# Clearing step 5's zero rows on VectorE, and a new order for the first batch

## The chip, the cores and the metric

The kernel runs on one core of a Trainium2 chip. The metric is the device time of one execution in microseconds (us), as a median of several runs. The core has five engines, each with its own queue of instructions that it works off in order: TensorE (PE), VectorE (DVE), ScalarE (ACT), GpSimd (POOL) and SyncE (SP). SP, ACT and POOL also issue transfers (DMAs) between the chip's memory and the core. An engine waits where the next instruction in its queue needs something that another engine or a transfer has not delivered yet.

## The reference

The program is an attention with normalised q and k, whose output goes through a layer of eight experts to which tokens are routed by a hash of their id.

```python
q_n = q / sqrt(mean(q*q) + 1e-6) * g_q        # q, k, v: 8 x 12 x 448 x 64
k_n = k / sqrt(mean(k*k) + 1e-6) * g_k
attn = softmax(q_n @ k_n^T / sqrt(64))
x = attn @ v                                   # as 3584 x 768
expert = token_id * 2654435761 % 8
out[mask_e] = relu(x[mask_e] @ w1[e]) @ w2[e]  # for each expert e
```

## The kernel before

Attention comes first, then the experts. Attention has 48 steps: eight batches of six, and each step takes two heads. The 448 tokens of a head lie as 64 rows of seven, and the two heads of a step share the 128 partitions. The seven groups of 64 keys of two heads make three full blocks of scores (j = 0, 1, 2) and a half one (j = 3).

Around the steps stands the preparation, by groups of steps. In the first batch, group 0 is step 0 alone, group 1 the pair of steps 1 and 2, group 2 the pair 3 and 4 and step 5 alone. The work is written as short tokens, `kind:step.part` or `kind:group.tensor`, that a Python loop turns into instructions. Nothing reorders them: each engine's queue is the order of the tokens that it takes part in. The kinds are:

- `sqq`, `sqk`: squares of q or k of a group. `sumq`, `sumk`: partial sums of them on PE. `redq`, `redk`: the rest of the sums on DVE. `ln`, `er`: two ACT operations that turn the sums into 1/rms, for k and q of a group together, or apart for group 0 (`ln:0.0.1` is q's, `ln:0.1.2` is k's).
- `nq`, `nk`: DVE multiplies q or k by 1/rms (lines 420 to 440). `Tq`, `Tk`: PE transposes the result into a PSUM bank. `qT`, `kT`: that bank is copied to SBUF, kT with the factor g_col.
- `sc`: scores on PE. `exp`: exponentials on ACT. `av`: product with v on PE, in three parts. `rec`, `x`: reciprocal of the row sums and the final product on DVE. `v`: a copy of a chunk of v on DVE.
- `zero`: clears rows that no load fills. `spin`: PE multiplies zeros, with no result used. `gain`: the factors g_q and g_k are made into g_col.

A suffix says who does it or where: `@A` puts a square or a copy on ACT instead of DVE; `@S` puts sums or transposes into a bank of the ring of three that the scores use, instead of the one bank of their own.

Odd heads leave holes in the blocks of a single step, so for steps 0 and 5 some rows of q and k are cleared. For step 5 `zero:3` does it on ACT, in two copies of zeros, and then issues six small loads on SP (four for k, two for q, in 32 bits, without a cast) and the load of the token ids. Step 0's k comes on SP's and ACT's queues; all other loads of q, k and v are issued by POOL in the order of its queue, and but for step 0's q they change 32 bits to 16.

The first string of tokens covers batch 0 and batch 1 up to `exp:12.2`; a second string, `steady`, is then emitted for each batch from 2 on and begins with `exp:12.3` for batch 2. The names in the rows: `first` is shown as expT, whose buffer it borrows; `raw(1, 5)` and `raw(0, 5)` are parts of kr and qr; `warm`, the zeros, is shown as hi.

Of the kernel before, what the change touches and what calls it, by code (L numbers as in the profile page):

```python
# [20 lines left out]
def kernel(  # L21
# [12 lines left out]
    nc = tc.nc  # L34

    B, H, S, D = q.shape
# [3 lines left out]
    P = 128  # L40
    HP = H // 2
# [87 lines left out]
    def setup1():  # L129
        tid_t32 = _dc.replace(moe_token_ids.tensor, shape=[N * 2], dtype=I32)  # L130
        nc.sync.dma_start(out=tid32[:],
                            in_=bass.AP(tensor=tid_t32, offset=0,
                                        ap=[[2 * NTC, P], [2, NTC], [1, 2]]))
# [130 lines left out]
    with tc.manual_schedule(), \  # L264
# [45 lines left out]
        def raw_at(bufs, b, o, n):  # L310
            o += RAW // 2 * (b % 2)
            return bufs[b // 2 % NB][:, o:o + n]
# [15 lines left out]
        def raw(a, s):  # L328
            b, i = s // HP, s % HP
            bufs = (q_bufs, k_bufs)[a]  # L330
            if s == 0:
                return first[:, a]
            if s == HP - 1:
                return raw_at(bufs, 0, 4 * PAIR, 16 * D).bitcast(FP32).rearrange(
                    "p (s d) -> p s d", d=D)
            if b == 0:
                t = raw_at(bufs, 0, (i - 1) * PAIR, 2 * PAIR)
                return t.rearrange("p (i s d) -> p i s d", i=2, d=D)
            t = raw_at(bufs, b, 0, 6 * PAIR).rearrange("p (i u s d) -> p u i s d", i=2, u=3, d=D)
            return t[:, i // 2]  # L340
# [107 lines left out]
        V = nc.vector  # L448
# [12 lines left out]
        warm = hi[:].rearrange("p c a h -> p (c a h)")[:, 0:512]  # L461
# [270 lines left out]
        def load_one(s):  # L732
            load_heads([nc.sync] * 4, raw(1, s)[:, None], k, s, 1)
            load_one_q([nc.sync] * 2, raw(0, s), s)

        def zero_q(eng, t):
            eng.memset(t[64:P, 3::4, :], 0.0)

        def zero_kv(eng, t, s0=0, s1=7):
            eng.memset(t[64:P, :, s0, :], 0.0)  # L740
            eng.memset(t[0:64, :, s1, :], 0.0)

        def zero(part):
            V = nc.vector
            if part == 0:
                zero_kv(V, first[:, 1:2])
                zero_q(V, first[:, 0])
            elif part == 1:
                V.memset(n8_one[:, 4, 1], 0.0)
                V.memset(n8_one[:, 8, 0], 0.0)  # L750
            elif part == 2:
                V.memset(n8_k[:, :, 0, 1], 0.0)
                V.memset(n8_k[:, :, 7, 0], 0.0)
            elif part == 3:
                z = warm[:, 0:4 * D].rearrange("p (s d) -> p s d", d=D)
                nc.scalar.copy(raw(1, HP - 1)[:, 0::7], z[:, 0:2])
                nc.scalar.copy(raw(0, HP - 1)[64:P, 3::4], z[64:P, 0:2])
                load_one(HP - 1)
                setup1()
            elif part == 6:  # L760
                zero_kv(V, v_bufs[0])
            elif part == 7:
                V.memset(v8_all[:, :, :, :, D], 1.0)
                V.memset(v8_all[64:P, :, :, 0, D], 0.0)
                V.memset(v8_all[0:64, :, :, 7, D], 0.0)
# [77 lines left out]
        def gain(part):  # L843
            if part == 1:
                pend["g"] = ps_sc.tile([P, 2, 512], FP32, name="sc_ps")[:, 1, 0:1]
            g_mul(part, pend.get("g"))

        setup_ops = {"zero": zero, "gain": gain, "spin": spin}

        flag = ""  # L850

        def emit(text, b):
            nonlocal flag
            g0, s0, c0 = (0, 0, 0) if b is None else (b + 3, HP * b, 2 * b)
            for token in text.split():
                kind, arg = token.split(":")
                kind, _, flag = kind.partition("@")
                at, *rest = [int(a) for a in arg.split(".")]
                if kind in setup_ops:
                    setup_ops[kind](at)  # L860
                elif kind in group_ops:
                    if g0 + at < NG:
                        group_ops[kind](g0 + at, *rest)
                elif kind == "v":
                    if c0 + at < NV:
                        prep_v(c0 + at)
                elif s0 + at < NS:
                    step_ops[kind](s0 + at, *rest)

        emit("""  # L870
            zero:0 zero:1 zero:2 zero:6 zero:7 spin:11 sqk:0.0 zero:3 sqq@A:0.0 sumk@S:0.0
            redk:0.0 sumq@S:0.0 ln:0.1.2 redq:0.0 er:0.1.2 ln:0.0.1 er:0.0.1 sqk@A:1.0
            gain:0 spin:2 nk:0 spin:4 gain:1 Tk@S:0 nq:0 sumk@S:1.0 gain:2 sqq:1.0 Tq@S:0
            redk:1.0 sumq:1.0 kT:0 redq:1.0 qT@A:0 sc:0.0 ln:1 er:1 sc:0.1 spin:5 exp:0.0
            nk:1 Tk@S:1 sc:0.3 nq:1 Tq:1 sqk:2.0.0 kT:1 qT:1 exp:0.1 sqq:2.0.0 v:0
            sqk@A:2.0.1 sc:0.2 exp:0.3 sumk@S:2.0 sc:1.0 sqq@A:2.0.1 exp:0.2 exp:1.0
            sumq:2.0 redk:2.0 av:0.0 redq:2.0 sc:1.2 av:0.1 v:1 sc:1.3 ln:2 er:2 av:0.2
            sc:1.1 nq:3 rec:0 exp:1.2 exp:1.3 Tq@S:3 exp:1.1 nk:3 sc:2.0 Tk:3 x:0 exp:2.0
            sc:2.1 exp:2.1 qT:3 kT:3 sc:2.2 av:1.0 exp:2.2 sc:2.3 av:1.1 av:1.2 sqk:3.0
            sc:4.0 exp:2.3 nk:5 sumk:3.0 rec:1 exp:4.0 sc:3.0 x:1 sc:3.1 av:2.0 redk:3.0  # L880
            av:2.1 sqk:4.0 exp:3.0 nq:5 sumk:4.0 v:2 sc:3.2 av:2.2 redk:4.0 sqq:3.0 rec:2
            exp:3.1 Tk@S:5 sc:3.3 kT:5 x:2 sumq:3.0 exp:3.2 sc:4.3 sc:4.2 exp:3.3 redq:3.0
            exp:4.3 ln:3 er:3 sc:4.1 exp:4.2 av:3.0 sqk:4.1 Tq:5 exp:4.1 sqq:4.0 av:3.1 qT:5
            sumk@S:4.1 nq:6 av:3.2 nk:6 redk:4.1 sc:5.0 rec:3 sumq:4.0 sc:5.3 sc:5.1 exp:5.0
            exp:5.3 redq:4.0 sqq:4.1 x:3 Tk:6 exp:5.1 Tq@S:6 kT:6 sumq@S:4.1 redq:4.1 qT@A:6
            av:4.0 av:4.1 ln:4 sc:5.2 av:4.2 er:4 exp:5.2 sc:6.0 sqk:5.0 v:4 sc:7.0 sumk:5.0
            exp:6.0 rec:4 sc:6.3 x:4 av:5.0 av:5.1 exp:7.0 exp:6.3 nq:8 sc:7.3 redk:5.0 nk:8
            exp:7.3 v:3 Tq:8 sc:6.1 av:5.2 qT:8 sc:6.2 Tk@S:8 rec:5 sqq:5.0 exp:6.1 sc:7.1
            sumq:5.0 x:5 exp:6.2 av:6.0 sc:7.2 exp:7.1 exp:7.2 kT:8 sc:8.0 sqq:5.1 redq:5.0
            sc:8.1 nq:10 exp:8.0 av:6.1 sumq:5.1 nk:10 redq:5.1 exp:8.1 av:6.2 sc:8.3 rec:6  # L890
            Tk:10 x:6 sc:9.0 sc:8.2 exp:8.3 av:7.0 sc:9.3 exp:9.0 kT:10 Tq:10 av:7.1 av:7.2
            sc:9.1 sqk:5.1 qT:10 exp:8.2 rec:7 sc:9.2 x:7 v:5 exp:9.3 exp:9.1 sumk:5.1
            redk:5.1 exp:9.2 sqq:6.0 av:8.0 av:8.1 av:8.2 sc:10.0 sc:10.2 sc:10.1 rec:8 ln:5
            er:5 x:8 nk:12 exp:10.0 sumq:6.0 av:9.0 exp:10.1 sc:10.3 redq:6.0 Tk:12 av:9.1
            nq:12 av:9.2 kT:12 rec:9 exp:10.2 sc:11.0 exp:10.3 exp:11.0 sc:11.2 exp:11.2
            sc:11.3 x:9 Tq:12 sqq:6.1 av:10.0 av:10.1 sc:11.1 qT:12 nk:14 av:10.2 exp:11.3
            sc:12.0 sumq:6.1 sc:12.2 rec:10 exp:11.1 sc:12.1 x:10 exp:12.0 exp:12.2 redq:6.1
            Tk:14 sc:12.3 sqk:6.0 exp:12.1
        """, None)
        steady = """  # L900
            exp:0.3 av:-1.0 av:-1.1 nq:2 av:-1.2 kT:2 sc:1.0 exp:1.0 rec:-1 x:-1 Tq:2 sc:1.1
# [22 lines left out]
    with tc.manual_schedule(), \  # L924
# [116 lines left out]
        V = nc.vector  # L1041
# [236 lines left out]
```

## Time and profile before

| | us |
|---|---|
| median of 3 runs (337.82 to 338.94) | 338.56 |
| the profiled execution | 337.33 |
| its span | 335.8 |
| ACT busy in the span | 188.2 |
| DVE busy in the span | 197.7 |
| start of the first exponential | 11.90 |
| start of the first exponential of the steady part (exp:12.3) | 53.97 |
| start of the last exponential of attention | 157.08 |

The profile is one execution, seen from its span's start at 0. Shares over the whole span mix two stages: attention up to about 158 us, the experts after it. In attention ACT is the engine that the rows show as busy without a break, in the experts it is PE. A row of the timeline is a run of like instructions on one engine: start, time from the first start to the last end, engine and line, operation, what it writes and reads, the shape, how many; in brackets the idle time of the engine just before, and what ended it.

### The profile page before, as it was taken

Reading aid. Unit: us, or ns where it says so; the run is one execution under the profiler, and the core shown is the slowest. Engines: PE = TensorE matmul, PEld = TensorE weight load, DVE = VectorE, ACT = ScalarE, POOL = GpSimd, SP = SyncE. Lnnn points to the kernel's source line nnn. Section 1 sums busy time; section 2 is a strip of 40 time slices with the busy share of each in tenths; the row PEclk is TensorE's granted clock in tenths of the full one; section 3 lists DMA queues with packets and bytes.
Section 4 is the critical chain, followed back from the end, with each engine's and each line's share of the span. In section 5 each row is a group of like instructions: output and inputs, shape, how many; then the busy total and the mean of one; then the engine's idle time right before and its main releaser. Section 6 shows DMA issues by size and latency. Waiting matters only on the chain. (4 is left out here: it accounts for less than half of the span.)

```text
span 335.8 us, 9161 instructions
## 1 busy us (share of the span) xinstructions
PE 322.8 (96%) x3873; PEld 224.9 (67%) x3873; DVE 197.7 (59%) x427; ACT 188.2 (56%) x287; POOL 147.0 (44%) x207
## 2 busy tenths in 40 slices
PE   6899999999999999998999999999999999999992
PEld 3567776777777776666677667677676676766761
DVE  4699999998989899984792342232332323222210
ACT  3799999999999999998442211212022020221211
POOL 8799925423440100003655844538556374203122
PEclk9999999999999999999999999999999999999997
DMA  6999999999999999432587899999999999923012
GB/s 118 205 202 204 214 228 197 242 200 237 203 243 210 248 227 236 84 84 72 156 169 224 162 209 247 264 280 247 255 262 263 268 254 265 267 34 133 25 64 105
DMA packets 45602, 65.54 MB, mean 195 GB/s; under 512 B 12727, under 2 KB 33423, under 8 KB 45432
## 3 DMA queue, kind: packets, MB, share of 16 engines
q0 software_dynamic: 39072, 58.32, 86.0%
q1 hardware_dynamic: 6328, 6.50, 7.2%
q8 instruction: 31, 0.51, 0.6%
q10 hardware_dynamic: 160, 0.11, 0.1%
q14 instruction: 11, 0.09, 0.1%
HBM read 89.29 MB, written 17.30 MB: 317 GB/s over the span
## 5 line engine op out<-in xcount | busy, mean ns | idle before, releaser
L652 ACT ACTIVATE expT<-sc_ps 128x896 bf16<-128x896 f32 x144 | 125.0, 960 | 0.9 <-PE sc_ps L636 0.6
L972 PEld LDWEIGHTS <-h_sb 128*128 128x128 f16 (+1 forms) x512 | 51.3, 104 | 30.2
L972 PE MATMUL o_ps<-w_sb,h_sb 128*128 128x512 f16 (+3 forms) x384 | 66.2, 326 | 0.0
L985 POOL DMA_INDIRECT out_dram<-o_sb,gidx x32 | 33.8, 1055 | 63.4 <-ACT o_sb L982 30.9
L959 ACT ACTIVATE h_sb<-h_ps 128x480 f16<-128x480 f32 (+1 forms) x36 | 19.9, 553 | 67.3 <-PE h_ps L955 67.3
L230 POOL DMA_INDIRECT kr<-x_scratch,gidx x32 | 32.7, 1022 | 50.8 <-DVE oc L578 36.7
L955 PEld LDWEIGHTS <-w_sb 128*128 128x128 f16 x288 | 38.9, 136 | 16.2
L955 PE MATMUL h_ps<-xT,w_sb 128*128 128x480 f16 x240 | 49.4, 366 | 0.0
L982 ACT COPY o_sb<-o_ps 128x768 f32<-128x768 f32 x16 | 12.8, 799 | 60.4 <-PE o_ps L972 55.2
L961 DVE TENSOR_SCALAR h_sb<-h_ps 128x480 f16<-128x480 f32 x28 | 18.4, 658 | 47.2 <-PE h_ps L955 47.2
L636 PE MATMUL sc_ps<-qT,kT 64*128 64x448 f16 x288 | 44.4, 356 | 0.7 <-DVE qT L628 0.4
L671 PEld LDWEIGHTS <-expT 128*128 128x128 bf16 x864 | 37.8, 97 | 9.0 <-DVE x_sb L702 4.1
L671 PE MATMUL av_ps<-v,expT 128*128 128x65 bf16 x846 | 42.3, 193 | 0.1
L982 DVE COPY o_sb<-o_ps 128x768 f32<-128x768 f32 (+1 forms) x15 | 14.3, 956 | 37.1 <-PE o_ps L972 30.3
L305 POOL DMA_DIRECT2D vr<-in_v_dram x36 | 23.7, 669 | 20.1 <-DMA kr<-in_k_dram 10.8
L702 DVE TENSOR_TENSOR x_sb<-av_ps,srec 128x448 f16<-128x448 f32 x47 | 29.2, 622 | 1.3
L655 ACT ACTIVATE expT<-sc_ps 128x448 bf16<-128x448 f32 x48 | 28.6, 599 | 0.1
L386 PEld LDWEIGHTS <-ident 128*128 128x128 f16 x576 | 22.6, 97 | 8.2 <-issue 3.6
L676 PE MATMUL av_ps<-v,expT 128*128 128x130 bf16 x141 | 24.5, 220 | 0.0
L972 PE MATMUL o_ps<-kr,h_sb 128*128 128x512 f16 (+3 forms) x128 | 21.6, 326 | 0.0
L243 DVE COPY xT<-xT_ps 128x768 f16<-128x768 f16 (+1 forms) x21 | 11.0, 524 | 17.9 <-PE xT_ps L242 17.7
L955 PE MATMUL h_ps<-xT,qr 128*128 128x480 f16 x96 | 19.8, 366 | 0.0
(218 smaller groups left out, 437.9 us busy)
## 6 DMA issues: line engine op xcount, KB each, us to landing
w_sb<-in_moe_w_dram POOLq DMA_DIRECT2D x18, 512.0 KB, 12.4
w_sb<-in_moe_w_dram POOLq DMA_DIRECT2D x8, 768.0 KB, 13.1
kr<-in_k_dram POOLq DMA_DIRECT2D x7, 672.0 KB, 14.9
qr<-in_q_dram POOLq DMA_DIRECT2D x7, 672.0 KB, 12.4
x_scratch<-x_sb SPq DMA_DIRECT2D x15, 288.0 KB, 6.8
w_sb<-in_moe_w_dram POOLq DMA_DIRECT2D x2, 1536.0 KB, 21.6
qr<-in_moe_w_dram POOLq DMA_DIRECT2D x6, 512.0 KB, 17.5
vr<-in_v_dram POOLq DMA_DIRECT2D x14, 192.0 KB, 13.1
```

The source lines that it names most:

```text
L230: nc.gpsimd.indirect_dma_start(out=xg[0:idx.shape[0], :], out_offset=None, in_=x_dram[0:rows, :], in_offset=bass.IndirectOffsetOnAxis(ap=i ...
L305: eng.dma_start(out=dst[64 * half:64 * half + 64, :, s0:s0 + cnt, :].rearrange("p n s d -> p n (s d)"), in_=runs(t, h0 + HP * hh, 1, n, to ...
L636: nc.tensor.matmul(sc[:, hh, :S], lhsT=kT[64 * hh:64 * hh + 64, P * j:P * j + P], rhs=qT[64 * hh:64 * hh + 64, :], start=True, stop=True)
L652: nc.scalar.activation(expT[:, 2 * j:2 * j + 2, :], sc[:, :, :S], AF.Exp, bias=0.0, scale=1.0)
L655: nc.scalar.activation(expT[:, 6, :], sc[:, 0, :S], AF.Exp, bias=0.0, scale=1.0)
L671: nc.tensor.matmul(av[:, 2 * t + hh, :], lhsT=expT[:, tl(hh, j), P * t:P * t + P], rhs=v8[:, i, vs(hh, j), 0:D + 1], start=(hh == 0 and t ...
L676: nc.tensor.matmul(av[:, 2 * t:2 * t + 2, :], lhsT=expT[:, 6, P * t:P * t + P], rhs=v8[:, i, 0::7, 0:D + 1], start=False, stop=False)
L702: nc.vector.tensor_tensor(out=xs[b][:, :, hp * D:hp * D + D], in0=av[:, :, :D], in1=srec[:, :, None].to_broadcast([P, SL, D]), op=ALU.mult)
L955: nc.tensor.matmul(h_ps[:, :c1 - c0], lhsT=w1v[:, co, fo, :], rhs=xT[:, co, c0:c1], start=(co == 0), stop=(co == CO - 1))
L972: nc.tensor.matmul(o_ps[d0 > 0][0:w, d0:d1], lhsT=h_sb[:, fo, col * P:col * P + w], rhs=w2_sb[:, fo, d0:d1], start=(fo == 0), stop=(fo == ...
L982: (nc.vector.tensor_copy if col % 2 else nc.scalar.copy)(o_sb[0:w], o_ps[0][0:w])
L985: scat = nc.gpsimd.indirect_dma_start(out=out[:, :], out_offset=bass.IndirectOffsetOnAxis(ap=idx[0:w], axis=0), in_=o_sb[0:w], in_offset=N ...
```

## The change

The two copies of zeros on ACT become two memsets on DVE. They stand where `zero:3` stands in the order, which is later than before, and the six small loads wait for them. The first string of tokens is written in another order, with the same tokens but for the spins (before 11, 2, 4 and 5; now 11, 8, 3 and 1), and with some of them on another engine or in another bank.

```diff
             elif part == 3:
-                z = warm[:, 0:4 * D].rearrange("p (s d) -> p s d", d=D)
-                nc.scalar.copy(raw(1, HP - 1)[:, 0::7], z[:, 0:2])
-                nc.scalar.copy(raw(0, HP - 1)[64:P, 3::4], z[64:P, 0:2])
+                V.memset(raw(1, HP - 1)[:, 0::7], 0.0)
+                V.memset(raw(0, HP - 1)[64:P, 3::4], 0.0)
                 load_one(HP - 1)
                 setup1()
...
-            zero:0 zero:1 zero:2 zero:6 zero:7 spin:11 sqk:0.0 zero:3 sqq@A:0.0 sumk@S:0.0
-            redk:0.0 sumq@S:0.0 ln:0.1.2 redq:0.0 er:0.1.2 ln:0.0.1 er:0.0.1 sqk@A:1.0
+            zero:0 zero:1 zero:2 zero:6 zero:7 spin:11 sqq@A:0.0 sumq@S:0.0 redq:0.0
+            sqk@A:0.0 ln:0.0.1 gain:0 er:0.0.1 sumk@S:0.0 gain:1 redk:0.0 ln:0.1.2 spin:8
+            er:0.1.2 zero:3 gain:2 nk:0 sqk@A:1.0 Tk:0 nq:0 Tq@S:0 kT@A:0 sumk@S:1.0 sqq:1.0
...
```

On ACT before the change were sqq:0.0, sqk:1.0, qT:0, sqk:2.0.1, sqq:2.0.1 and qT:6; now there are sqq:0.0, sqk:0.0, sqk:1.0, kT:0, qT:0, sqk:2.0.1, kT:3, kT:5 and kT:6. The others of these kinds are on DVE.

ACT's queue from the last pair of ln and er of group 0 to the fifth full exponential (a minus is the order before, a plus the order now):

```order
 L411 ACTIVATE rr<-ss 128x16
 L372 ACTIVATE sq_k<-kr_68 128x14x16x4
+L622 ACTIVATE kT<-qkT_ps,g_col 128x512
 L622 ACTIVATE qT<-sc_ps 128x448
 L405 ACTIVATE ss<-ss 128x2x14
 L411 ACTIVATE rr<-ss 128x2x28
-L652 ACTIVATE expT<-sc_ps 128x896 x2
+L652 ACTIVATE expT<-sc_ps 128x896 x3
+L655 ACTIVATE expT<-sc_ps 128x448
 L372 ACTIVATE sq_k<-kr_68 128x8x16x4
-L655 ACTIVATE expT<-sc_ps 128x448
-L372 ACTIVATE sq_q<-qr_67 128x8x16x4
```

kT of step 0 is new on ACT, all four exponentials of step 0 stand ahead of the Square of step 5's k (128x8x16x4), and the Square of step 5's q has left ACT.

DVE's queue before, from the first Square of k (step 0) to the norms of steps 1 and 2:

```order
L374 TENSOR_TENSOR sq_k<-expT 128x8x16x4
L401 TENSOR_REDUCE ss<-sc_ps 128x8 x2
L190 MEMSET one_74 1x1
L191 TENSOR_TENSOR grow<-grow 1x128
L434 TENSOR_TENSOR n_one<-expT,rr 128x2x4x64 x2
L195 COPY g_col<-sc_ps 128x1
L374 TENSOR_TENSOR sq_q<-qr_67 128x14x16x4
L401 TENSOR_REDUCE ss<-sc_ps 128x14
L625 TENSOR_SCALAR kT<-sc_ps,g_col 128x512
L401 TENSOR_REDUCE ss<-qkT_ps 128x14
```

And DVE's queue now, from the second reduction of step 0 to kT of steps 1 and 2:

```order
L401 TENSOR_REDUCE ss<-sc_ps 128x8
L755 MEMSET kr_68 128x2x64
L756 MEMSET qr_67 64x2x64
L195 COPY g_col<-sc_ps 128x1
L434 TENSOR_TENSOR n_one<-expT,rr 128x2x4x64 x2
L374 TENSOR_TENSOR sq_q<-qr_67 128x14x16x4
L401 TENSOR_REDUCE ss<-sc_ps 128x14 x2
L434 TENSOR_TENSOR n_q<-qr_67,rr 128x2x7x64
L434 TENSOR_TENSOR n_k<-kr_68,rr 128x2x7x64
L443 COPY v_145<-vr_143 128x8x64
L628 COPY qT<-qkT_ps 128x896
L625 TENSOR_SCALAR kT<-sc_ps,g_col 128x1024
```

The two memsets, for which SP's small loads wait, stand behind the second reduction and ahead of g_col; the Square of k of step 0 and the kT of step 0 are gone from DVE. After the rows shown come the Squares of steps 3 and 4 and then, as sq_q 128x8x16x4, that of step 5's q.

## Rows read from the trace of the kernel before

**Rows 1.** Stretches: us, each engine's busy time (instructions), clock, DMA, GB/s
```profile
22.66:53.97 31.31, 31.31 (x622) 23.31 (x617) 30.71 (x68) 30.92 (x48) 21.79 (x51) 1.00 1.34 211
60.00:100.00 40.00, 39.99 (x742) 29.27 (x741) 37.05 (x79) 40.00 (x61) 14.40 (x21) 1.00 1.30 222
```

**Rows 2.** Timeline of ACT, start-up and last exponential of attention
```profile
5.72 0.63 ACT L372 ACTIVATE sq_q<-expT 128x512 f16<-128x512 f32 x1 [2.60 <-DMA expT<-in_q_dram]
8.35 0.95 ACT L372 ACTIVATE sq_k<-kr 128x896 f16<-128x896 f16 x1 [0.36 <-DMA kr<-in_k_dram]
10.18 0.54 ACT L622 ACTIVATE qT<-sc_ps 128x448 f16<-128x448 f16 x1 [0.88 <-PE sc_ps L601]
11.49 0.23 ACT L405 ACTIVATE ss<-ss 128x28 f32<-128x28 f32 x1 [0.76 <-DVE ss L401]
...
11.90 1.71 ACT L652 ACTIVATE expT<-sc_ps 128x896 bf16<-128x896 f32 x2
...
16.25 0.92 ACT L652 ACTIVATE expT<-sc_ps 128x896 bf16<-128x896 f32 x1 [0.36 <-PE sc_ps L636]
...
157.08 0.74 ACT L655 ACTIVATE expT<-sc_ps 128x448 bf16<-128x448 f32 x1
```

**Rows 3.** Timeline of ACT, 19 to 54 us
```profile
19.05 3.34 ACT L652 ACTIVATE expT<-sc_ps 128x896 bf16<-128x896 f32 x4
22.24 0.59 ACT L655 ACTIVATE expT<-sc_ps 128x448 bf16<-128x448 f32 x1
22.66 3.40 ACT L652 ACTIVATE expT<-sc_ps 128x896 bf16<-128x896 f32 x4
...
31.13 0.94 ACT L622 ACTIVATE qT<-sc_ps 128x896 f16<-128x896 f16 x1
...
53.97 0.61 ACT L655 ACTIVATE expT<-sc_ps 128x448 bf16<-128x448 f32 x1
```

**Rows 4.** Timeline of DVE, start-up
```profile
1.76 0.17 DVE L737 MEMSET expT<- 64x128 f32 x1
...
5.57 0.69 DVE L374 TENSOR_TENSOR sq_k<-expT 128x512 f16<-128x512 f32 x1 [1.69 <-DMA expT<-in_k_dram]
6.91 0.19 DVE L401 TENSOR_REDUCE ss<-sc_ps 128x8 f32<-128x32 f32 x1 [0.64 <-PE sc_ps L386]
...
7.63 1.28 DVE L434 TENSOR_TENSOR n_one<-expT,rr 128x512 f16<-128x512 f32 x2
...
9.95 0.63 DVE L374 TENSOR_TENSOR sq_q<-qr 128x896 f16<-128x896 f16 x1 [0.97 <-DMA qr<-in_q_dram]
...
10.62 0.47 DVE L625 TENSOR_SCALAR kT<-sc_ps,g_col 128x512 f16<-128x512 f16 x1
...
14.31 0.74 DVE L625 TENSOR_SCALAR kT<-sc_ps,g_col 128x1024 f16<-128x1024 f16 x1
```

**Rows 5.** Timeline of PE, start-up
```profile
7.12 1.29 PE L791 MATMUL av_ps<-hi 128*128 128x448 f16 x6
...
9.76 0.38 PE L601 MATMUL sc_ps<-ident,n_one 128*128 128x128 f16 x4
```

**Rows 6.** Timeline of SP's queue: the small loads of step 5
```profile
3.59 2.42 SPq L305 DMA_DIRECT2D kr<-in_k_dram  x4
...
6.76 0.61 SPq L299 DMA_DIRECT2D qr<-in_q_dram  x1
```

**Rows 7.** Transfers of narrow windows: size, us to landing; last, a queue at 10:11
```profile
expT<-in_q_dram POOLq DMA_DIRECT2D x1, 96.0 KB, 3.3
kr<-in_k_dram SPq DMA_DIRECT2D x2, 48.0 KB, 4.6
qr<-in_q_dram SPq DMA_DIRECT2D x1, 96.0 KB, 5.9
vr<-in_v_dram POOLq DMA_DIRECT2D x1, 96.0 KB, 7.8
q1 hardware_dynamic: 141, 0.12, 49.2%
```

More of the change, by code (lines that the diff above doesn't have):

```diff
@@ L870 @@
         emit("""
-            zero:0 zero:1 zero:2 zero:6 zero:7 spin:11 sqk:0.0 zero:3 sqq@A:0.0 sumk@S:0.0
-            redk:0.0 sumq@S:0.0 ln:0.1.2 redq:0.0 er:0.1.2 ln:0.0.1 er:0.0.1 sqk@A:1.0
[L873 to L898, printed above, removed]
+            zero:0 zero:1 zero:2 zero:6 zero:7 spin:11 sqq@A:0.0 sumq@S:0.0 redq:0.0
+            sqk@A:0.0 ln:0.0.1 gain:0 er:0.0.1 sumk@S:0.0 gain:1 redk:0.0 ln:0.1.2 spin:8
+            er:0.1.2 zero:3 gain:2 nk:0 sqk@A:1.0 Tk:0 nq:0 Tq@S:0 kT@A:0 sumk@S:1.0 sqq:1.0
@@ new lines @@
+            qT@A:0 redk:1.0 sumq@S:1.0 sc:0.0 redq:1.0 ln:1 sc:0.1 sc:0.2 er:1 nq:1 exp:0.0
+            nk:1 v:0 spin:3 spin:1 Tq:1 qT:1 exp:0.1 Tk@S:1 kT:1 sqk:2.0.0 sc:0.3 exp:0.2
+            exp:0.3 av:0.0 sc:1.0 sqq:2.0.0 sqk@A:2.0.1 sc:1.1 exp:1.0 sc:1.2 sumk:2.0
+            exp:1.1 sqq:2.0.1 av:0.1 sumq@S:2.0 redk:2.0 exp:1.2 av:0.2 v:1 redq:2.0 sc:2.0
+            v:2 rec:0 ln:2 er:2 nk:3 sc:2.2 x:0 sc:1.3 Tk:3 exp:2.0 nq:3 nq:5 exp:1.3 sc:2.3
+            av:1.0 exp:2.2 sqk:3.0 av:1.1 Tq@S:3 qT:3 sc:2.1 exp:2.3 kT@A:3 Tq@S:5 exp:2.1
@@ new lines @@
+            av:1.2 rec:1 qT:5 x:1 sc:4.0 sumk:3.0 exp:4.0 nk:5 sc:3.0 exp:3.0 sc:4.1 av:2.0
+            redk:3.0 av:2.1 sqk:4.0 Tk@S:5 sumk:4.0 sqq:3.0 exp:4.1 sc:3.1 redk:4.0 kT@A:5
+            exp:3.1 sqk:4.1 av:2.2 rec:2 sumq:3.0 redq:3.0 sc:3.2 exp:3.2 sumk@S:4.1 sc:3.3
+            ln:3 sqq:4.0 sumq:4.0 x:2 exp:3.3 redk:4.1 er:3 sc:4.2 redq:4.0 sc:5.0 sqq:4.1
+            sc:4.3 av:3.0 nk:6 sumq:4.1 v:3 exp:4.2 av:3.1 redq:4.1 exp:4.3 nq:6 exp:5.0
+            av:3.2 rec:3 ln:4 x:3 sc:5.3 sqk:5.0 Tk:6 exp:5.3 er:4 Tq@S:6 av:4.0 qT:6 sc:5.2
@@ new lines @@
+            kT@A:6 exp:5.2 nk:10 sc:5.1 av:4.1 av:4.2 sc:6.0 nq:8 sc:7.0 sumk:5.0 exp:5.1
+            exp:6.0 Tq@S:8 rec:4 x:4 redk:5.0 av:5.0 exp:7.0 sc:6.3 nk:8 av:5.1 exp:6.3
+            sc:7.2 qT:8 sc:7.1 sc:6.2 exp:7.2 sqq:5.0 sqk:5.1 av:5.2 rec:5 sumq:5.0 exp:7.1
+            Tk@S:8 redq:5.0 sumk:5.1 sqq:5.1 sc:6.1 redk:5.1 exp:6.2 kT:8 sc:7.3 sumq:5.1
+            x:5 exp:6.1 sc:8.0 exp:7.3 redq:5.1 nq:10 sc:8.2 av:6.0 Tk:10 exp:8.0 av:6.1
+            ln:5 av:6.2 exp:8.2 sc:9.0 sc:8.1 v:4 kT:10 er:5 sc:9.2 exp:9.0 rec:6 Tq:10 x:6
@@ new lines @@
+            av:7.0 exp:8.1 sqq:6.0 av:7.1 qT:10 exp:9.2 nq:12 sc:8.3 sc:9.1 av:7.2 rec:7
+            sumq:6.0 x:7 redq:6.0 nk:12 sc:10.0 exp:8.3 sc:10.2 exp:9.1 Tq:12 sc:9.3 sqq:6.1
+            exp:10.0 exp:10.2 av:8.0 av:8.1 qT:12 exp:9.3 av:8.2 sc:10.1 sc:11.0 exp:10.1
+            rec:8 Tk:12 x:8 sc:10.3 av:9.0 av:9.1 av:9.2 kT:12 rec:9 x:9 exp:11.0 sc:11.2
+            sc:11.1 sumq:6.1 exp:10.3 sqk:6.0 sc:11.3 av:10.0 v:5 exp:11.2 av:10.1 sc:12.0
+            exp:11.1 exp:11.3 redq:6.1 nk:14 av:10.2 sc:12.1 exp:12.0 rec:10 exp:12.1
@@ L899 @@
+            sc:12.2 x:10 Tk:14 exp:12.2 sc:12.3
         """, None)
```

## The prediction

> **What bounds the kernel now.** I read the table of stretches first, then ScalarE's timeline, then the rows of whoever it waits for. ScalarE (ACT) is busy in all of 60 to 100 us, and its exponentials follow one another up to the last of the 48 steps at 157.8 us [rows 1, 2]. The reader is to see that no other engine ends a wait of ACT in that stretch, so whatever is lost or won on ACT before 54 us arrives at the end one for one. The change touches only what lies before exp:12.3, the exponential that starts at 53.97 us and is the 52nd [rows 3]. So the question is one number: when does that exponential start? I call the time by which its start moves D.
>
> I count ACT in slots, the distance between two starts. A full exponential (128x896) has 0.80 us: four start at 19.05 and the next instruction at 22.24. A short one (128x448) has 0.42, from 22.24 to 22.66 [rows 3]. Neighbours overlap by about 0.15 us, since the last of those four ends 0.15 after the next start. A slot is therefore a duration less 0.15: 0.48 for a Square of 512 (0.63) and 0.79 for qT:6 (0.94). A pair of ln and er has 0.41 (11.49 to 11.90) [rows 2, 3].
>
> **The change part by part.** *The zero rows.* ACT's two casts go. They ended before the first load had arrived, in the 2.60 us for which ACT then waits at 5.72 [rows 2], so they are worth nothing. Two memsets go to VectorE (DVE), about 0.17 each by the nearest form [rows 4]. They stand behind both first reductions and ahead of g_col's copy and the first norms, in a time when DVE waits for ACT's er anyway; uncovered they would cost 0.3 us, and below zero they cannot be.
>
> What the move does to SyncE (SP) is larger. The six small loads of step 5, and the token ids behind them, now wait for those memsets. The first small load was issued at 3.59, the sixth at 6.76 [rows 6]; the memsets end near 8.0 (below), so all go out 4.4 us later, the last k load near 9.8, the last q load near 11.15. Nothing else is in SP's queue until x is stored.
>
> *Start-up, walked in the new order.* Squares of step 0: q at 5.72 as before, for it waits for the same load; k now behind it on ACT, 6.20 to 6.87, where DVE did it beside ACT. From the end of a Square to the start of its reduction on DVE it took 0.65 us (6.26 to 6.91 for the old k [rows 4]), so q's reduction now comes near 7.0 and k's near 7.5. Then ln and er for k end near 8.2, and DVE, which has done the memsets by 8.0, writes k's and q's norms at 8.24 and 8.84, 0.60 apart as before (two in 1.28 us [rows 4]), the last done near 9.5.
>
> TensorE (PE) meanwhile has eight spins in a row. Six took 1.29 us [rows 5], 0.20 each, so eight from 7.8 end at 9.4: Tk:0 waits 0.4 us for them. Tq:0 then ends near 10.14, where it ended before (9.76 plus 0.38 [rows 5]). kT:0 and qT:0 both run on ACT, 10.0 and 10.45, and end near 11.0; before, kT:0 ended on DVE at 11.09, because it stood behind a Square that waited 0.97 us for q's load [rows 4]. So scores start near 11.05 instead of 11.15 and the first exponential near 11.8 instead of 11.90. Should q's pair load land as late as before (9.95) it is 11.9; with the small loads out of its way, 11.6.
>
> From there ACT runs all four exponentials of step 0 (3 x 0.80 + 0.42 = 2.82) and one Square (0.5): exp:1.0 can start at 15.1, against 16.25 before, where ACT had two Squares of group 2 in between and waited 0.36 us for PE [rows 2]. Scores of step 1 are due by then: its norms follow er:1 on DVE near 12.0, and five operations of 0.55 us later, v:0 among them, kT:1 ends near 14.7. The Square needs step 5's k: 9.8 plus 4.6, the median of two of the four k loads [rows 7], gives 14.4 against 14.6. I charge nothing.
>
> *The next wait.* Three exponentials later, at 17.5, ACT comes to ln:2. It needs the sums of q of group 2, and those need sqq:2.0.1, now on DVE and waiting for the last small q load; PE stands behind it in its own order with the sums, then av:0.2 and the scores of step 2. From landing to ln:2 it is about 1.8 us (Square 0.6, sums 0.8, reduction and hand-overs 0.4). The landing is 11.15 plus L. L is not known in the new place: from below the 3.3 us of a q load that met an idle start, from above the 7.8 us of a v load issued at 8.86; the same load took 5.9 in the crowd of 6.8 to 12.7, when the hardware queue carried 0.12 MB in one us beside the software queue [rows 7]. I take 5.0, between the small k loads (4.6) and its own 5.9: landing at 16.15, ln:2 at 17.95. At 3.3 ACT never waits; at 7.8 it waits until 20.75. DVE's copy of the third v chunk also moves up, to about 17.8; its first load lands at 8.86 + 7.8 = 16.7 [rows 7], so I charge nothing.
>
> After ln:2 and er:2 (to 18.4) come exp:2.0, 1.3, 2.2, 2.3 (2.44), then kT:3 on ACT, then exp:2.1. I add 0.2 and 0.3 for scores that now stand behind transposes of step 3, whose norms are late on DVE too. kT of 1024 columns has no row on ACT: it lies above qT's 0.94 for 896, and by that row's and the 448 row's slope (0.40 for 448 columns) at 1.05, slot 0.90; one of 512 has 0.45. Bounds: 0.79 and, were it dearer by as much again as the step from 896 to 1024, 1.0. So the 13th exponential starts at 18.4 + 2.44 + 0.2 + 0.90 + 0.3 + 0.80 = 23.04, against 22.66 [rows 3]: 0.38 later.
>
> The Trainium skill bears on that slot (ScalarE: Activation LUTs, section "What ACT_TABLE_LOAD costs"). An ACTIVATE takes 186 ns plus 0.833 ns per column, and a per-partition pointer operand adds about 93 ns. The trace agrees for the immediate form: 0.94 for 896 [rows 3]. kT's scale is the pointer g_col, which no row of ACT here shows; by the page the three kT after the first exponential would cost 0.28 us more, and D would be 0.7 instead of 0.4.
>
> *The rest of the first batch.* ACT has kT:5 (0.45) and kT:6 (0.90) more and qT:6 (0.79) less: 0.56. Against it, DVE loses kT:3, 5 and 6 (0.74, 0.47, 0.74) and gains one Square (0.69) and qT:6, a narrower copy that is no dearer than 0.74 [rows 4]: at least 0.5 us less in all. That matters only through gaps: between 22.66 and 53.97 ACT has 30 full and 9 short exponentials, qT:6 and three pairs, 24.0 + 3.8 + 0.8 + 1.3 = 29.9 of 31.3 us, so 1.4 us are lost in gaps while DVE is busy for 30.71 of 31.31 us [rows 1]. Between none and all of it could come back; I take 0.5.
>
> Sum: D = 0.38 + 0.56 - 0.5 = +0.44 us. The profiled execution took 337.33 (span 335.8 and 1.5 around it), 1.2 less than the median of 338.56; I add D to the median: **339.0 us**. About 0.3% (1.0 us) is what a measurement here can tell from no change, so I forecast none.
>
> **The rivals.** *Late q load, slower.* Place: sqq:2.0.1 on DVE with PE behind it. With the old 5.9 us the load lands at 17.05 and ln:2 starts at 18.85, 0.9 later; if the gaps also stay, because DVE then is behind again, D = 0.44 + 0.9 + 0.5 = 1.8, **340.4**. It decides from a landing near 16.7 on. For it: the load's own row, and that the queues ahead are fuller after 11 us. Against: in the old place it waited for its own turn behind four other loads as well. With 7.8 D is about 3.
>
> *Freed start, faster.* The small loads' 459 KB (q and k of two heads, 448 x 64 numbers of 4 bytes) leave the stretch before 10 us, so the pair loads land sooner and exp:0.0 starts at 11.5 (0.3 less), the small loads land in time (0.4 less) and the gaps close by 0.6 more: D = -0.9, **337.7**. For it: ACT waited 0.36 and DVE 0.97 us for just these pair loads [rows 2, 4]. Against: the new chain goes through ACT twice and through eight spins before it needs them.
>
> *DVE is the bound.* If the 98% of DVE and not ACT's order sets the first batch, ACT's new work is free and DVE's 0.5 us come off: **338.1**. Against: from 60 to 100 us the same steps run with ACT busy throughout and DVE for 93% [rows 1], and DVE's 98% may be work that waited for ACT.
>
> **How the numbers follow.** Forecast 0.48, late load 0.30, freed start 0.14, DVE bound 0.08. Over 0.3% faster: most of the freed start (0.10), half of the DVE case (0.04), 0.01 of the forecast: 0.15. Over 0.3% slower: 0.27 of the late load and 0.05 of the forecast (where kT's slot and the gaps fall badly): 0.32. The rest, 0.53, is no change. The range reaches down to the freed start with a little more, 337.4, and up to a late load between 5.9 and 7.8, 341.0; the forecast's own is 338.3 to 339.9.
>
> **What would show it.** Right: exp:0.0 near 11.8; no wait of ACT on PE before exp:1.0, which starts near 15.1; a short wait at ln:2 put down to DVE or PE, and DVE waiting for the qr load just before sqq:2.0.1; four kT on ACT of 0.6 to 1.1 us; exp:12.3 near 54.4; from there the same distances. Wrong: spins longer than 0.20 us, so that Tk:0 starts after 10; a small k load that ACT waits for; or a start of exp:12.3 that moves and an end that does not move with it.

## The result, and the profile after

| | median, us | runs | ratio to the kernel before (95%) |
|---|---|---|---|
| before, beside it | 338.66 | 8 | |
| changed | 340.71 | 8 | 1.0058 [1.0037, 1.0079] |
| before, later session | 337.72 | 22 | |
| changed, later session | 341.12 | 6 | 1.0121 [1.0088, 1.0153] |

The changed kernel is slower, by 0.6% in one session and 1.2% in the other. The ratios are those on record, taken over the fast runs (the first session's without one run of 344.66 us), and are not the quotients of the two medians, which are 1.0061 and 1.0101. The forecast was 339.0, no change. The time lies in the range, but only because the largest rival, the late q load at 340.4, was in it; that rival's mechanism is the one that came true. The forecast's own 338.3 to 339.9 does not hold 340.71.

There are two profiled executions of the changed kernel. In the first (344.66 us) the granted clock of TensorE was 0.50 for most of the stretch from 18 to 30 us. The second (339.85 us, the shortest of its six runs) shows the change without that, so I read it first. ScalarE's timeline in it answers to [rows 2, 3]; the last line is exp:12.3:

```profile
13.11 2.52 ACT L652 ACTIVATE expT<-sc_ps 128x896 bf16<-128x896 f32 x3
...
16.65 0.63 ACT L372 ACTIVATE sq_k<-kr 128x512 f16<-128x512 f32 x1 [0.59 <-issue]
17.19 2.51 ACT L652 ACTIVATE expT<-sc_ps 128x896 bf16<-128x896 f32 x3
20.29 0.24 ACT L405 ACTIVATE ss<-ss 128x44 f32<-128x44 f32 x1 [0.58 <-DVE ss L401]
...
23.18 1.14 ACT L622 ACTIVATE kT<-qkT_ps,g_col 128x1024 f16<-128x1024 f16 x1
24.18 3.37 ACT L652 ACTIVATE expT<-sc_ps 128x896 bf16<-128x896 f32 x4
...
56.43 0.56 ACT L655 ACTIVATE expT<-sc_ps 128x448 bf16<-128x448 f32 x1
```

exp:12.3 starts at 56.43 instead of 53.97 [rows 3]: D is 2.46 where 0.44 was forecast. ln:2 (20.29) waits for DVE. VectorE's timeline of the same execution says why, and SP's queue (the four k loads, then q's two) has the cause; they answer to [rows 4, 6]:

```profile
7.48 0.17 DVE L755 MEMSET kr<- 128x128 f32 x1
7.73 0.17 DVE L756 MEMSET qr<- 64x128 f32 x1
...
16.32 0.62 DVE L374 TENSOR_TENSOR sq_q<-qr 128x896 f16<-128x896 f16 x1
18.41 0.69 DVE L374 TENSOR_TENSOR sq_q<-qr 128x512 f16<-128x512 f32 x1 [1.48 <-DMA qr<-in_q_dram]
```

```profile
7.67 2.43 SPq L305 DMA_DIRECT2D kr<-in_k_dram  x4
10.15 1.00 SPq L298 DMA_DIRECT2D qr<-in_q_dram  x1
11.19 1.35 SPq L299 DMA_DIRECT2D qr<-in_q_dram  x1
```

The last load of q is issued at 11.19, as forecast (11.15), but its Square can start only at 18.41, 2.26 later than the forecast landing (16.15).

The first execution has the same waits in larger form. ScalarE, then TensorE's clock by stretches (length; busy us and instructions of PE, PEld, DVE, ACT, POOL; granted clock, DMA share, GB/s), then that last q load (KB, us to landing):

```profile
11.54 2.52 ACT L652 ACTIVATE expT<-sc_ps 128x896 bf16<-128x896 f32 x3
...
16.03 0.63 ACT L372 ACTIVATE sq_k<-kr 128x512 f16<-128x512 f32 x1 [1.55 <-DMA kr<-in_k_dram]
...
21.27 0.24 ACT L405 ACTIVATE ss<-ss 128x44 f32<-128x44 f32 x1 [2.19 <-DVE ss L401]
...
60.36 0.56 ACT L655 ACTIVATE expT<-sc_ps 128x448 bf16<-128x448 f32 x1
```

```profile
19.00:28.00 9.00, 7.82 (x80) 5.41 (x80) 6.15 (x12) 5.11 (x9) 8.21 (x23) 0.50 1.37 202
```

```profile
qr<-in_q_dram SPq DMA_DIRECT2D x1, 96.0 KB, 7.3
```

TensorE's rows, of the first execution and then of the second:

```profile
16.71 0.79 PE L386 MATMUL qkT_ps<-sq_k,ident 128*128 128x88 f16 x16 [1.38 <-ACT sq_k L372]
...
19.60 1.35 PE L386 MATMUL sc_ps<-sq_q,ident 128*128 128x88 f16 x16 [1.65 <-DVE sq_q L374]
```

```profile
7.75 3.15 PE L790 MATMUL av_ps<-hi 128*128 128x448 f16 x8
...
17.34 0.79 PE L386 MATMUL qkT_ps<-sq_k,ident 128*128 128x88 f16 x16 [0.59 <-ACT sq_k L372]
...
19.16 0.80 PE L386 MATMUL sc_ps<-sq_q,ident 128*128 128x88 f16 x16 [0.59 <-DVE sq_q L374]
```

In the first, TensorE stood idle for 1.38 and 1.65 us before its two sums of group 2 and then ran at the lower of its two levels; that execution's D is 6.39, against 2.46 in the second, where the clock stayed at 1.00 after 12 us. The fall is not apart from the late loads: in the second execution the first exponential came 1.57 us later (the eight spins there took 3.15 us), and so TensorE waited only 0.59 us for each of the same two sums.

The mean granted clock of every run is on record. Of the 14 runs of the changed kernel the five with the lowest, 0.980 to 0.988, are also the five longest, 341.43 to 344.66 us; the other nine took 339.53 to 341.09. None of the twelve runs of the first experiment below, with the loads early, is under 0.993. So part of the measured loss goes with a lower clock in some of the runs, which the second execution does not show.

One number for the frame: the profiled time less the start of exp:12.3 is 337.33 - 53.97 = 283.36 before, 339.85 - 56.43 = 283.42 now, and 283.2 to 283.5 in the other seven experiments of the first two sessions of experiments, in which exp:12.3 lies anywhere from 53.60 to 60.1. So D arrives at the end one for one. It is 284.3 in the first execution of the changed kernel, and 284.1 to 284.3 in the four experiments of the last session, which ran on another chip.

### The profile page after: what moved, and what is told of

The parts are those of the page before. It is cut to its first block, busy times and chain, and to the rows that moved or that the text cites. A ratio compares the mean times of both kernels' runs of the same rounds, so it can differ in the third digit from the quotient of the medians.

```text
span 343.1 us, 9164 instructions
## 1 busy us (share of the span) xinstructions
PE 327.2 (95%) x3874; PEld 227.9 (66%) x3874; DVE 197.9 (58%) x426; ACT 190.2 (55%) x288; POOL 147.0 (43%) x207
## 5 line engine op out<-in xcount | busy, mean ns | idle before, releaser
L671 PEld LDWEIGHTS <-expT 128*128 128x128 bf16 x864 | 38.6, 98 | 9.5 <-DVE x_sb L702 3.6
```

The lines of the kernel that those rows point to most:

```text
L671: nc.tensor.matmul(av[:, 2 * t + hh, :], lhsT=expT[:, tl(hh, j), P * t:P * t + P], rhs=v8[:, i, vs(hh, j), 0:D + 1], start=(hh == 0 and t ...
```

## The experiments

Theory: the small loads, q's last of all, land later than forecast because they are issued later, and ln:2 with the rest of ACT waits for them. Rivals: the new order with its copies on ACT costs the time; TensorE's clock does; the memsets do.

**Loads early again.** The changed kernel with `zero:3` back near the front.

```diff
- zero:0 zero:1 zero:2 ... er:0.1.2 zero:3 gain:2
+ zero:0 zero:1 zero:3 zero:2 ... er:0.1.2 gain:2
```

> The changed kernel, with the two memsets and the six small loads put back to the start (second in VectorE's order of zeros), everything else in the new order. Theory 1 (the loss is the late small loads): ACT waits neither before the Square of step 5's k nor at ln:2, exp:1.0 starts near 15.2, the steady part near 53.5 to 54, and the time is 337.7 to 338.7, no slower than before. Theory 2 (the loss is the new order, with ACT's extra copies): the time stays near 340.5.

Measured: 338.15 against 337.84, ratio 1.0004 [0.9986, 1.0021]. The loss is gone. ScalarE in it:

```profile
13.10 2.51 ACT L652 ACTIVATE expT<-sc_ps 128x896 bf16<-128x896 f32 x3
...
18.86 0.26 ACT L405 ACTIVATE ss<-ss 128x44 f32<-128x44 f32 x1
...
22.77 3.37 ACT L652 ACTIVATE expT<-sc_ps 128x896 bf16<-128x896 f32 x4
...
55.03 0.56 ACT L655 ACTIVATE expT<-sc_ps 128x448 bf16<-128x448 f32 x1
```

The first exponential starts where it did in the changed kernel's second execution (13.10 and 13.11). ln:2 is 1.43 earlier and waits for nothing, and exp:12.3 is 1.40 earlier: the late loads' price in these two executions. It is 0.4% of the time, less than the 0.6 and 1.2% measured over the runs.

**Old order, loads late.** The order of before, memsets on DVE, the loads behind `redq:0.0`.

```diff
- sqk:0.0 zero:3 sqq@A:0.0 ... redq:0.0 er:0.1.2
+ sqk:0.0 sqq@A:0.0 ... redq:0.0 zero:3 er:0.1.2
```

> The kernel before, in its old order, with the two memsets on VectorE and the six small loads put behind the second reduction of step 0, so that they go out near 7.8 us. Theory 1 (late loads): ACT itself waits for both small Squares, about 2.5 us for k's and then for q's until 18.8, exp:1.0 starts near 20.5 instead of 16.25, time 341.5 to 343. Theory 2 (the order): near 338.7.

Measured: 340.38, ratio 1.0085 [1.0063, 1.0107]; exp:12.3 at 56.17, 2.20 later than before. ACT waits for both loads itself:

```profile
15.71 0.63 ACT L372 ACTIVATE sq_k<-kr 128x512 f16<-128x512 f32 x1 [1.79 <-DMA kr<-in_k_dram]
...
17.53 0.63 ACT L372 ACTIVATE sq_q<-qr 128x512 f16<-128x512 f32 x1 [0.76 <-DMA qr<-in_q_dram]
```

The 341.5 to 343 that was expected did not come: the waits were 1.79 and 0.76 us, not 2.5 for k alone. But late loads cost about as much in the old order as in the new one, and by both tests it is the loads.

**Copies back on DVE.** The first experiment, with kT of steps 3, 5 and 6 on DVE.

```diff
- kT@A:3 ... kT@A:5 ... kT@A:6
+ kT:3 ... kT:5 ... kT:6
```

> As the run with the loads early, and kT of steps 3, 5 and 6 copied by VectorE again instead of ACT. Theory 1 alone says nothing here; my sum priced the three copies at 2.25 us of ACT's slots. If they stand on the path, this run is 1 to 2 us faster than the one with early loads alone; if VectorE, busy for 98%, is the bound, it is as fast or up to 1 us slower.

Measured: 339.25, ratio 1.0045 [1.0028, 1.0063]; exp:12.3 at 56.25, 1.22 after the first experiment's. ACT now waits for scores that stand behind kT:

```profile
22.45 0.92 ACT L652 ACTIVATE expT<-sc_ps 128x896 bf16<-128x896 f32 x1 [0.50 <-PE sc_ps L636]
23.99 2.60 ACT L652 ACTIVATE expT<-sc_ps 128x896 bf16<-128x896 f32 x3 [0.62 <-PE sc_ps L636]
...
33.27 3.35 ACT L652 ACTIVATE expT<-sc_ps 128x896 bf16<-128x896 f32 x4 [0.81 <-PE sc_ps L636]
```

The copies on ACT are a gain in this order, not its cost. The likely reason, argued and not shown, is that DVE has little time left for them: it is busy for 30.6 of the 32.2 us from 22.8 to 55.

**Spins in the wait.** The changed kernel with ten more spins before the q sums of group 2.

```diff
+ for _ in range(10): nc.tensor.matmul(both[:, 1, 0:448], lhsT=warm[:, 0:P], rhs=warm[:, 0:448], ...)
```

> The changed kernel, late loads and all, with ten more multiplications of zeros on PE just before the sums of q of group 2, where PE waits for the late load. Theory 3 (the granted clock falls because PE stands still there, and PE then runs at the lower of its two levels until about 30 us): the clock stays at 1.0 from 12 to 36 us and the time falls by 0.5 to 2 us against the changed kernel, to 339 to 340. If the clock costs nothing: 340.7, unchanged, since ACT's wait for the load stays.

Measured: 342.01, ratio 1.0111 [1.0081, 1.0140]; exp:12.3 near 60.1. TensorE had already stood idle for 2.72 us ahead of k's sums; the ten spins behind them took 3.57 us, at a granted 0.59 in 19 to 23 us, and only stood in front of q's sums. A miss; it doesn't isolate what the clock costs.

**The changed kernel again**, unaltered; its profile is the second execution above.

> The changed kernel once more, unaltered, for a second profile. In the first, PE's granted clock was 0.5 from 18.7 to 29 us, and the steady part began at 60.36. Theory 1 (late loads): the two waits, 1.5 us before the Square of step 5's k and 2.2 us at ln:2, are there again whatever the clock, and with the clock at 1.0 the steady part begins near 56 to 57. Theory 3 (the clock does it): with the clock at 1.0 it begins near 54.

Measured: 341.12, ratio 1.0121 [1.0088, 1.0153], with the granted clock at 1.00 from 12 to 30 us in the profile. The loss doesn't need the fall of the clock: this execution is still 2.1 us above the 337.72 of the kernel before. Its two waits, 0.59 and 0.58 us, are shorter than the expected 1.5 and 2.2.

**Two spins for eight.** The first experiment with `spin:2` for `spin:8`.

```diff
- spin:8
+ spin:2
```

> As the run with the small loads early, with two spins instead of eight ahead of Tk:0. In that run's profile the eight spins met a granted clock of 0.5 from 8.0 to 11.4 us and ended near 10.2 instead of 9.2, so that exp:0.0 started at 13.10 instead of 11.54. If that costs what it shows, Tk:0 now starts near 9.05, exp:0.0 near 11.3 to 11.6, and the time is 0.5 to 1.5 us below that run's, 336.8 to 337.6 against 337.8 of the kernel before. If the spins keep the clock up, it falls more often and the time is the same or up to 1 us longer.

Measured: 338.44, ratio 1.0022 [1.0009, 1.0035]; exp:0.0 at 11.95 instead of 13.10, but exp:12.3 at 54.49, 0.54 earlier only, and no better time. The granted clock was 0.50 in 10 to 12 us. The hoped-for 1 us did not come.

**Late loads, less company.** The changed kernel, with POOL issuing batch 1's first loads only behind its own clearing and set-up.

```diff
- load(1)
- load(2, "kq")
  zero_kv(nc.gpsimd, v_bufs[1])
  ...
  setup2()
+ load(1)
+ load(2, "kq")
```

> The changed kernel, loads late, with batch 1's big loads issued by POOL after its own set-up work (about 7 us later), so that fewer transfers of the software queue are under way from 11.5 to 18 us. For the time the small loads take: by my argument (the crowd beside them stretches them from 5 to 7.3 us) the last q load lands within 4 to 5.5 us of its issue, and ACT's wait at ln:2 is under 0.5 us; if they take 7 us again, it is not the crowd after 11.5. The kernel's time is not of interest: batch 1's squares will wait for their data.

Measured, in one execution: 343.16. Batch 1's first k load was issued at 18.42 instead of 11.53. The k loads took 6.2 to 7.5 us all the same and the last q load 7.2, so in this execution batch 1's loads are not what slows them; steps 3 and 4 and v still filled the software queue. The start-up was the faster one here, TensorE's clock stayed at 1.00, and ln:2 was no earlier for it:

```profile
11.52 2.51 ACT L652 ACTIVATE expT<-sc_ps 128x896 bf16<-128x896 f32 x3
...
20.53 0.24 ACT L405 ACTIVATE ss<-ss 128x44 f32<-128x44 f32 x1 [0.72 <-DVE ss L401]
```

Besides, batch 1's k then came too late itself:

```profile
36.52 0.92 DVE L374 TENSOR_TENSOR sq_k<-kr 128x1344 f16<-128x1344 f16 x1 [0.92 <-DMA kr<-in_k_dram]
```

**Only the memsets.** The order of before, loads early, clearing on DVE instead of ACT.

```diff
- nc.scalar.copy(raw(1, HP - 1)[:, 0::7], z[:, 0:2])
- nc.scalar.copy(raw(0, HP - 1)[64:P, 3::4], z[64:P, 0:2])
+ V.memset(raw(1, HP - 1)[:, 0::7], 0.0)
+ V.memset(raw(0, HP - 1)[64:P, 3::4], 0.0)
```

> The kernel before, in its old order, with only the form of the clearing changed: two memsets on VectorE among its first zeros instead of two copies on ACT, the loads going out at 3.6 us as before. All theories: no change, 337.5 to 338.2 against 337.8; a difference would price the memsets themselves.

Measured: 337.39 against 337.72, ratio 0.9996 [0.9979, 1.0012]. Who clears costs nothing that shows here; when the loads go out does.

**More spins at the start.** The first experiment, and the one just told, with fourteen spins for eleven.

```diff
- spin:11
+ spin:14
```

> The changed order with the small loads early (as in the first experiment) and fourteen spins instead of eleven at the very start, so that TensorE's idle of about 1.05 us at 5.2 to 6.3 is filled. Theory: the eight spins before the first transposes took 2.80 us instead of 1.6 because the granted clock had fallen after that idle time; with the gap filled the clock stays at 1.00, the eight spins take about 1.6 us, the first exponential starts at about 11.6 to 12.0 instead of 13.1, exp:12.3 at about 53.6 to 54.2 instead of 55.03, and the time is 0.8 to 1.4 us under the first experiment's 338.15: about 337.0, ratio to the kernel before 0.995 to 0.998. Rival: the clock falls in some executions whatever stands there; then the time is as in the first experiment, 338.1 to 338.4, ratio 1.000 to 1.001, and rows at half clock show again between 8 and 12 us.

> The old order with only the memsets on VectorE (loads early, median 337.39 there, ratio 0.9996) and fourteen spins at the start instead of eleven. That kernel already had only 0.36 us of idle TensorE before the sums of k. Both theories: exp:0.0 near 11.0 to 11.6 (the added spins may delay the first sums by up to 0.8 us), time 337.2 to 338.0, ratio 0.999 to 1.001. If this one is clearly faster than 0.997, the clock at the start costs the kernel before something too in most executions.

Measured: new order 338.94 against 338.71, 0.9994 [0.9975, 1.0014]; old order 338.36, 0.9985 [0.9965, 1.0005]. In the new order the start-up did what the theory said: TensorE's eight spins took 1.69 us, and the first exponential came at 11.98 instead of 13.10. But exp:12.3 came at 54.89, 0.14 earlier than without it. VectorE, then ScalarE, show where the 1.12 us went:

```profile
31.68 0.86 DVE L374 TENSOR_TENSOR sq_k<-kr 128x1344 f16<-128x1344 f16 x1 [0.65 <-DMA kr<-in_k_dram]
```

```profile
11.98 2.51 ACT L652 ACTIVATE expT<-sc_ps 128x896 bf16<-128x896 f32 x3
...
35.69 0.54 ACT L655 ACTIVATE expT<-sc_ps 128x448 bf16<-128x448 f32 x1 [0.42 <-PE sc_ps L639]
36.44 2.54 ACT L652 ACTIVATE expT<-sc_ps 128x896 bf16<-128x896 f32 x3 [0.21 <-PE sc_ps L636]
39.19 0.92 ACT L652 ACTIVATE expT<-sc_ps 128x896 bf16<-128x896 f32 x1 [0.22 <-PE sc_ps L636]
...
54.89 0.56 ACT L655 ACTIVATE expT<-sc_ps 128x448 bf16<-128x448 f32 x1
```

DVE now waits for batch 1's first k, 672 KB on POOL's queue. In the new order exp:12.3 follows this Square by 23.2 to 23.3 us in every profile with these copies (33.18 to 56.43 in the changed kernel, 31.78 to 55.03 in the first experiment, 31.68 to 54.89 here). In this execution the faster start-up only moved the wait to this transfer. Whether the filled idle time kept the clock up is not settled: the eight spins took 1.69 us as well in the changed kernel's first execution and in three experiments without the added spins (spins in the wait, less company, q early), after 0.76 to 0.95 us of idle TensorE. They took 2.80 to 3.17 us in four other executions, after 0.47 to 1.22 us. So the idle time does not tell the two cases apart.

**k early, q late; q early, k late.** `zero:3` taken apart: k's memset and loads, and as `zero:8` q's memset, loads and the token ids. In the first `zero:3` goes to the front and `zero:8` to the late place, in the second the other way round.

```diff
- er:0.1.2 zero:3 gain:2
+ zero:1 zero:3 zero:2 ... er:0.1.2 zero:8 gain:2
```

> The changed order with the four small k loads at the early place and only the two small q loads (and the token ids) at the late one, behind q's memset. They then find SP's queue empty and are issued at about 8.0 and 8.8 instead of 10.2 and 11.4. Theory (the landing of the small loads sets ln:2): with 6 to 7 us to landing q lands at 15 to 16, Square on DVE by 16.7, sums by 17.8; ln:2 waits not at all or up to 0.3 us; ACT does not wait for k; time 338.1 to 338.5, ratio 1.000 to 1.002. Rival (any small load issued that late costs the whole loss, by what it collides with in the queues): ratio 1.005 to 1.009 as in the changed kernel.

> The changed order with the two small q loads early and the four small k loads at the late place. I charged nothing for k in the prediction; in the changed kernel ACT waited 0.63 us for k ahead of exp:1.0, in a second execution not at all. If the last k load lands at about 16 (issued at 9.6 to 9.8, 6 to 6.8 us to landing), ACT waits for it before exp:1.0 by 0.3 to 0.7 us where the first exponential starts near 11.5, and not where it starts near 13.1, and ln:2 follows in order: time 338.2 to 339.0, ratio 1.000 to 1.003. If instead k alone holds the loss, ratio 1.005 to 1.009. If q alone holds it, ratio 1.000.

The first of the two did not do what it was made for. Its q loads went out at 6.05 and 6.75, before q's memset, as SP's queue and VectorE show:

```profile
6.05 0.66 SPq L298 DMA_DIRECT2D qr<-in_q_dram  x1
6.75 0.61 SPq L299 DMA_DIRECT2D qr<-in_q_dram  x1
```

```profile
7.89 0.17 DVE L758 MEMSET qr<- 64x128 f32 x1
```

q's loads don't touch the rows that the memset clears, so nothing makes them wait for it. It is the first experiment over again (1.0005 [0.9983, 1.0027]), and it says something about the changed kernel: there q's loads are late only because they stand behind k's in SP's queue, and k's wait for k's memset. Of the six small loads that the text ahead of the result has waiting for the memsets, only k's four do.

The second did: k at 7.74, q at 3.59. Measured 339.28, ratio 1.0016 [0.9996, 1.0036], and ACT waits for neither:

```profile
12.41 2.51 ACT L652 ACTIVATE expT<-sc_ps 128x896 bf16<-128x896 f32 x3
14.80 0.56 ACT L655 ACTIVATE expT<-sc_ps 128x448 bf16<-128x448 f32 x1
15.24 0.64 ACT L372 ACTIVATE sq_k<-kr 128x512 f16<-128x512 f32 x1
```

With k issued as late as in the changed kernel and only q early, most of the loss is gone: it sits in q's loads, behind k's. What is left in this execution, exp:12.3 at 55.36 against the first experiment's 55.03, comes after DVE's wait for batch 1's k:

```profile
32.16 0.86 DVE L374 TENSOR_TENSOR sq_k<-kr 128x1344 f16<-128x1344 f16 x1 [0.38 <-DMA kr<-in_k_dram]
```

That k alone costs nothing isn't shown by it, since the two of k's loads whose landing the trace has took 5.8 us there, where in the changed kernel's second execution the same two took 6.0 and 6.8.

## Where the prediction held and where it failed, step by step

| | forecast | changed, 2nd execution | loads early |
|---|---|---|---|
| first exponential | 11.8 | 13.11 | 13.10 |
| exp:1.0 | 15.1 | 17.19 | 16.44 |
| Square of the last q load | 16.15 | 18.41 | no wait |
| ln:2 | 17.95 | 20.29 | 18.86 |
| 13th exponential | 23.04 | 24.98 | 23.57 |
| exp:12.3 | 54.4 | 56.43 | 55.03 |

*The step that failed* is the landing, "I take 5.0". The chain was right: the memsets ended at 7.90, the last q load was issued at 11.19, Square, sums, reduction and ln:2 follow in 1.88 us (1.8 forecast). L measured 7.1 and 7.3 in the two executions, above the 5.9 of the old place [rows 7] and near the 7.8 kept as the upper bound. I had taken the middle between small k loads and q's own row, though the queues after 11 us were known to be fuller. No profile has this load at 5.0 or less: it took 5.3 to 6.9 us in its old place (eight profiles) and 6.4 to 7.3 in the late one (five). The rival "Late q load" named place and condition. With L = 7.1 and all else as forecast, the prediction's own sum gives ln:2 at 20.05, D = 2.54 and 341.1; measured are 20.29, 2.46 and 340.71 or 341.12.

Some of the agreement is luck. The rival's 340.4 is near because two errors of it offset each other: its L of 5.9 was too short, and its 0.5 for gaps that stay did not come. The issue at 11.19 came right because the k loads went out at 7.67, 0.33 before the forecast 8.0, while the issue of the q load before it took 1.00 us instead of 0.66.

In the balance below the load is 1.43, beside 0.91 for the start-up. That split holds for this execution only, since ln:2 starts when the later of two chains is done, ACT's own work or q's load. With the start-up as forecast ACT would only have waited longer: with less company the first exponential came at 11.52 and ln:2 at 20.53.

*k, charged nothing.* The forecast landing was 14.4; ACT waited for k until 16.03 in the first execution, since k's loads took 5.3 to 6.7 us instead of 4.6. In the second they took 6.0 to 7.1, and the same Square starts at 16.65 after 0.59 us of idle that the profile puts to nothing. The last of the four, issued near 9.5 with 7.1 us to landing, came in near 16.6, so this is a wait for k too. At ln:2, which needs q as well, this is inside q's wait: ACT waits there once more, for 2.19 and 0.58.

*Start-up.* The changed kernel's two profiles show two outcomes, 11.5 and 13.1; the forecast's 11.8 was near the first. By the time of ln:2 the later one is worth 0.91 (18.86 in the first experiment less 17.95). "Wrong: spins longer than 0.20 us" is what the later one shows: eight took 3.15 us in the second execution, 1.69 in the first. Before, six took 1.29 [rows 5]. The clock had no term in my sum.

*After ln:2.* The two waits for scores (0.2 and 0.3) did not come: -0.5. kT's slot of 1024 columns was 1.00 (23.18 to 24.18), not 0.90: the bound, +0.1. The Trainium skill (ScalarE: Activation LUTs, section "What ACT_TABLE_LOAD costs") had it right: by its terms, pointer operand included, the estimate is 1.13 us and for 512 columns 0.71. These runs show 1.10 to 1.15 and 0.69 to 0.76.

Together 0.38 + 0.91 + 1.43 - 0.5 + 0.1 = 2.32, the shift of the 13th exponential (24.98 - 22.66). *The rest of the batch* was to add 0.06 and added 0.14 (0.15 in the first experiment). So that term held.

*The rivals.* "Late q load": shown, by the first and second experiments and the last. "Freed start": its first half is there, the pair of q came in without a wait in the changed kernel and exp:0.0 at 11.54 in the first execution, but it bought nothing. "DVE is the bound": with the copies moved back to DVE the kernel lost 0.3% against the first experiment, which fits a DVE that sets the first batch as soon as it is given more; its 0.5 us less did not come back as time.

*The forecast's core.* Without the late loads the new order measured 1.0004, 1.0022, 0.9994 and 1.0005; the 0.13% that D = 0.44 stands for lies in the interval of each, and no change in all but the second's. No version here is shown to beat the kernel before; the old order with DVE's memsets (0.9996, 0.9985) comes nearest.

*Open.* Why the two sessions differ by 0.6% for the same kernel; two of the eight runs of the first and three of the six of the second have the low mean clock of 0.988 or less, which may be part of it. Why L grew: batch 1's loads are not needed for it, by one execution; leaving away those of steps 3 and 4 and v was not tried. And the profiled execution of before (337.33) lies below all three runs shown with it, so D, taken against it, is up to 1.2 us more than against a run at the median. The first experiment shows as much: its exp:12.3 is 1.06 later than in that profile, at a ratio of 1.0004.

## What to carry to other kernels

When an instruction on which loads wait is moved, walk the whole issuing queue behind it: the load that hurt here did not depend on the moved memset at all, it stood behind four that did. Where a transfer's time to landing is unknown in its new place, take the nearest row in time and crowd, not the middle of kinder ones, when a consumer has only a microsecond of slack. And a start-up that is made faster pays only as far as the next transfer allows.

## What the runs showed of the hardware that was not expected

- The time to landing of one and the same small load of 96 KB spread from 5.3 to 7.3 us: 5.5 issued at 4.3 (one profile), 5.3 to 6.9 at 6.8 (eight), 6.4 to 7.3 at 11.1 to 11.4 (five). Later was longer on the whole, but the ranges overlap. The issue itself took 0.61 to 0.63 us on SP in the nine early cases and 0.74 to 1.52 in the five late ones.
- The granted clock fell in one execution of the changed kernel after idle times of 1.38 and 1.65 us and stayed at 0.50 from 19 to 28 us, though TensorE was busy for 7.82 of those 9 us. It fell too after 2.72 us (spins in the wait). It did not fall after 0.59 and 0.59 (the second execution), nor after 1.43 and 0.73 (less company). In these four profiles it goes with the longer waits; that they are its cause is not shown.
- In the second execution eight spins took 3.15 us, 0.39 apart, while the row of that stretch shows the clock at 1.00. The trace of that execution has no clock record before 10.74 us, so the 1.00 is no measurement there: a stretch's granted clock can miss what the durations show.
